# Recurrent-memory attention with a squared-ReLU feed-forward: both score masks leave TensorE

## The chip, the cores and the metric

The kernel runs on one core of a Trainium2 chip. A core has five engines with instruction queues of their own, each working in order: TensorE (PE in the profile, with its weight loads as PEld), VectorE (DVE), ScalarE (ACT), GpSimd (POOL) and SyncE (SP), which issues DMAs here. The metric is the device time of one execution in microseconds (us), lower is better; the times shown are medians of several runs.

## The reference, cut to what matters

The sequence has 2048 tokens of width 640. It is cut into 64 segments of 32 tokens, and a memory of 8 rows is carried from each segment to the next. There are 32 heads of size 128.

```python
mask = (idx[:, None] < M) | (idx[:, None] >= idx[None, :])   # idx over M + 32 = 40 rows
for s in range(n_seg):
    h = concatenate([mem, xs])                 # 8 memory rows, 32 token rows
    q, k, v = h @ Wq, h @ Wk, h @ Wv           # per head
    scores = where(mask, q @ k.T * scale, -1e9)
    o = softmax(scores) @ v @ Wo
    mem = o[:M]                                # to the next segment
    outs.append(o[M:])
h = x + concatenate(outs)                      # xs came from layernorm(x)
out = h + (relu(layernorm(h) @ w1 + b1) ** 2) @ w2 + b2
```

A memory row (the first 8 queries) sees all 40 keys; a token row sees the 8 memory keys and the tokens up to its own. Since the memory rows of a segment are the output of the one before, the 64 segments form a chain.

## The kernel before

The function `step(b, sp)` computes one segment; it is called 64 times (16 blocks of 128 tokens, 4 segments each), and then the feed-forward part follows in 4 passes of 512 tokens. All instructions are issued in the order in which the code is written, so each engine's queue is the order of the calls. Work that does not depend on the memory (projections of token rows that were known beforehand, layer norms, output projections of earlier segments) sits in lists (`fill`, `late`, `mid`, `win`) from which `run` takes pieces at fixed places of a step.

The 40 rows of a segment are handled in two parts. 32 rows, the 8 memory rows and the first 24 tokens, go through the step's own projections (`hT4`, M = 8 and HD = 24). The last 8 tokens of every segment (TL = 8, the tails) are projected elsewhere, four segments at a time, since they need not wait for the memory. `tails_in` copies their queries and keys, as columns 32 to 39, into `qT` and `kT` on POOL. In `kT` the tail's 8 keys stand four times behind one another, so that a head has 64 key columns.

The heads are worked on in four groups `g` at once: group g uses 32 partitions of the output, and four small matmuls stand side by side on TensorE. n = 0, 1 are the two halves of the heads, j = 0 to 3 the heads within group and half.

**Memory rows** (`scores`, `soft1`, `soft2`, `values`): `qz` holds, for each head, 32 query columns of which only the head's own 8 are not zero. So the 16 matmuls of `scores(n)` add up four heads' scores in one PSUM tile `sm` of 128 partitions: partition 32 g + 8 j + m is memory row m of head j in group g. The first 32 of the 64 columns are the step's own keys; the last 32 hold the tail's keys four times. Four further matmuls of an identity with `bmask` (L416) put minus 1e9 on three of the four copies, so that a row keeps copy j alone. `soft1` takes the maximum and the exponential with its sum over 64 columns (`mx`, `em`, `zm`); `soft2` takes the reciprocal `rm`, multiplies (`pm`, named pmem in the profile) and transposes 32 x 32 blocks (`pT`, named pTm). After that, copy j of the tail's probabilities lies on the partitions where the tail values of head j lie (`vt4`), and `values(n)` multiplies both parts with v and vt4 (L449, L454).

**Token rows** (`token_scores`): 32 matmuls of 40 columns write the scores of all heads into one PSUM tile `skv` of 128 x (8 x 40). Ahead of them, four matmuls of 256 columns of an identity with `mask` (L489) write the causal mask. DVE takes the maximum (L525) and subtracts it (L527), ACT takes the exponential `ek` (L542), DVE sums and takes the reciprocal (L544, L546), POOL multiplies (L548, L551), and DVE and POOL bring the result into the form (`pTk`, `pTx`) in which the next step's `token_values` uses it.

The order within a step, on TensorE: projections q0, k0, q1, k1 (L206); memory scores of half 0; 8 matmuls of the value projection's half 0; token scores of half 0; the other 12 matmuls of value half 0, which ACT then copies to `v` (L502); 8 of value half 1; memory scores and token scores of half 1; `values(0)`; the other 12 of value half 1; output projection of the memory rows and earlier tokens (`wo_rounds`, L238) with `token_values` and `values(1)` in between. On ACT stand behind each other: the copy `oT` (L215), `ek`, and `otmp` (L245); on DVE the sum `zk`, `rk` and then `o` (L246). `otmp` and `o` add up the output projection, and `mem_to_hT` (L316, L318) brings the memory rows to the next step.

PSUM tiles `sm`, `pw` and `pm` share one buffer (pool `chn`); `skv` and the projections share three (pool `mm`).

Of the kernel before, what the change touches and what calls it, by code (L numbers as in the profile page):

```python
# [8 lines left out]
ACT = mybir.ActivationFunctionType  # L9
ALU = mybir.AluOpType  # L10
AX = mybir.AxisListType
F32 = mybir.dt.float32
BF16 = mybir.dt.bfloat16
# [3 lines left out]
def kernel(  # L17
# [16 lines left out]
    nc = tc.nc  # L34
# [3 lines left out]
    SEG = 32  # L38
# [45 lines left out]
    nc.vector.memset(mhalf[:], -0.5)  # L84
    mask = const.tile([128, HG, SEG], BF16)
    nc.vector.memset(mask[:], 0.0)
    nc.gpsimd.affine_select(out=mask[0:32], in_=mask[0:32], compare_op=ALU.is_ge, fill=NEG, base=0,
                            pattern=[[0, HG], [-1, SEG]], channel_multiplier=1)
    bmask = const.tile([128, 4, TL], BF16)
    qz = const.tile([128, H, 32], BF16)  # L90
# [8 lines left out]
    nc.vector.tensor_copy(out=same[:], in_=diag[:].unsqueeze(2).to_broadcast([128, 4, TL]))  # L99
    nc.vector.tensor_scalar(out=bmask[:], in0=same[:], scalar1=-1.0, scalar2=-NEG, op0=ALU.add, op1=ALU.mult)  # L100
    qT = const.tile([128, H, NK], BF16)
    kT = const.tile([128, H, 2 * SEG], BF16)
    oT = const.tile([128, H, NK], BF16)
# [216 lines left out]
    def tails_in(b, sp, which="qk", h0=0, h1=H):  # L320
        q, k = [tails[b][w][:].rearrange("p h (k s) -> p h s k", s=4)[:, h0:h1, sp, :] if w in which else None for w in "qk"]
        if "q" in which:
            nc.gpsimd.tensor_copy(out=qT[:, h0:h1, SEG:NK], in_=q)
        if "k" in which:
            nc.gpsimd.tensor_copy(out=kT[:, h0:h1, SEG:2 * SEG].rearrange("p h (j k) -> p h j k", k=TL),  # L325
                                  in_=k.unsqueeze(2).to_broadcast([128, h1 - h0, 4, TL]))

# [52 lines left out]
    def step(b, sp, v=None):  # L380
# [32 lines left out]
        def scores(n):  # L413
            sm = chn.tile([128, 512], F32, tag="ch", name="sm")
            for g in range(G):
                nc.tensor.matmul(sm[32 * g:32 * g + 32, SEG:2 * SEG], lhsT=ident[:, 0:32],  # L416
                                 rhs=bmask[:].rearrange("p j k -> p (j k)"), start=True, stop=False, skip_group_check=True)
            for j in range(4):
                for g in range(G):
                    p = n * 16 + g * 4 + j  # L420
                    nc.tensor.matmul(sm[32 * g:32 * g + 32, 0:2 * SEG], lhsT=qz[:, p, :], rhs=kT[:, p, :],  # L421
                                     start=False, stop=(j == 3), skip_group_check=True)
            sms[n] = sm

        def soft1(n):
            mx = s2.tile([128, 1], F32, tag="mx", name="mx")
            nc.vector.tensor_reduce(out=mx[:], in_=sms[n][:, 0:2 * SEG], op=ALU.max, axis=AX.X, negate=True)
            em = s2.tile([128, 2 * SEG], BF16, tag="em", name="em")
            zm = s2.tile([128, 1], F32, tag="zm", name="zm")
            nc.scalar.activation(out=em[:], in_=sms[n][:, 0:2 * SEG], func=ACT.Exp, bias=mx[:, 0:1], scale=1.0,  # L430
                                 accum_out=zm[:])
            ems[n], zms[n] = em, zm

        def soft2(n):
            rm = s2.tile([128, 1], F32, tag="rm", name="rm")
            nc.vector.reciprocal(out=rm[:], in_=zms[n][:])
            pm = s2.tile([128, 2 * SEG], BF16, tag="pmem", name="pmem")
            nc.vector.tensor_scalar(out=pm[:], in0=ems[n][:], scalar1=rm[:, 0:1], scalar2=None, op0=ALU.mult)
            pT = s2.tile([128, 2 * SEG], BF16, tag="pTm", name="pTm")
            nc.vector.transpose(out=pT[:], in_=pm[:])  # L440
            return pT
# [44 lines left out]
        def token_scores(n):  # L486
            if n == 0:
                for g in range(G):
                    nc.tensor.matmul(skv[32 * g:32 * g + 32, :, M:NK], lhsT=ident[:, 0:32], rhs=mask[:],  # L489
                                     start=True, stop=False, skip_group_check=True)  # L490
            for j in range(4):
                for g in range(G):
                    nc.tensor.matmul(skv[32 * g:32 * g + 32, n * 4 + j, :], lhsT=qT[:, n * 16 + g * 4 + j, M:NK],  # L493
                                     rhs=kT[:, n * 16 + g * 4 + j, 0:NK], start=False, stop=(n == 1 and j == 3),
                                     skip_group_check=True)
# [26 lines left out]
        if not last:  # L522
            pT1 = soft2(1)
        mxk = s1.tile([128, HG], F32, tag="mxk", name="mxk")
        nc.vector.tensor_reduce(out=mxk[:], in_=skv, op=ALU.max, axis=AX.X)  # L525
        tk = s1.tile([128, HG, NK], F32, tag="tk", name="tk")
        nc.vector.tensor_tensor(out=tk[:], in0=skv, in1=mxk[:].unsqueeze(2).to_broadcast([128, HG, NK]), op=ALU.subtract)  # L527

# [370 lines left out]
```

## Time and profile before

| | us |
|---|---|
| median of the runs | 1021.12 |
| runs, lowest and highest | 1020.16, 1023.35 |
| the profiled execution | 1020.98 |
| its span, first to last instruction | 1018.8 |
| PE busy | 972.1 |
| DVE busy | 621.6 |
| ACT busy | 533.8 |
| POOL busy | 309.3 |

The granted clock of TensorE was 0.996 of full speed over the span. Views of the trace used here: the page; the chain of work that ended last, in order of time (each row: start, duration, engine, tile, line, how many); the timeline (start, duration, engine, line, operation, output and inputs, shapes; in brackets the engine's idle time ahead of it and what ended it); the groups by line and shape (busy us in all, mean ns of one, idle time ahead); and the waits (waiting engine, tile and line, then whom it waited for: us in all, times, longest). Matmuls overlap, and their ends are modelled, so PE's busy time includes short waits. The 64 segments take most of the span, the weights' loading some 50 us at the start, and the feed-forward part the last 140 or so.

### The profile page before, as it was taken

To read this page: it belongs to the slowest core of one execution; us is meant where nothing else is said; L and a number is where in the kernel's file an instruction comes from. 1 tells how busy PE (TensorE), PEld (TensorE's weight loads), DVE (VectorE), ACT (ScalarE), POOL (GpSimd) and SP (SyncE) were. 2 spreads that over 40 slices of the span, in tenths; PEclk is the share of its full clock that TensorE was granted. 3 is DMA by queue.
4 is the path that set the end of the run, shared out by engine and by line. 5 is a ranking of instruction groups with operands and counts; after the bars stand their busy time and mean duration, and the time that the engine had idled before them with its cause. 6 is when DMAs were issued, how large, how long until landed. Compare 5 with 4: busy or idle time off the path is not lost.

```text
span 1018.8 us, 58958 instructions
## 1 busy us (share of the span) xinstructions
PE 972.1 (95%) x26951; PEld 582.4 (57%) x26960; DVE 621.6 (61%) x1740; ACT 533.8 (52%) x1229; POOL 309.3 (30%) x803
## 2 busy tenths in 40 slices
PE   5789899999999999999999999999999998999998
PEld 2345555655655755656655666556566565555565
DVE  2256676767666667566667666666666676466432
ACT  3335555565555555555555555555555555533431
POOL 2023333333333333323333332323232343433210
PEclk9999999999999999999999999999999999999999
DMA  9960101000101010000000000000000110612200
GB/s 362 398 190 21 23 7 30 8 24 7 35 7 30 7 38 11 27 10 27 15 21 16 24 19 15 22 14 28 15 22 8 48 35 6 212 48 66 78 26 26
DMA packets 39112, 51.57 MB, mean 51 GB/s; under 512 B 5968, under 2 KB 35024, under 8 KB 36944
## 3 DMA queue, kind: packets, MB, share of 16 engines
q1 hardware_dynamic: 38080, 47.48, 14.1%
q8 instruction: 210, 3.44, 1.4%
q10 hardware_dynamic: 784, 0.34, 0.1%
q14 instruction: 38, 0.31, 0.1%
HBM read 38.37 MB, written 9.44 MB: 47 GB/s over the span
## 4 chain that ended last, share of the span: by engine, by line
PE 88%; DMA 6%; DVE 2%; issue 1%; ACT 1%; SPq 0%; DVEq 0%; POOL 0%; ACTq 0%; POOLq 0%
PE ps L206 48%; PE pw L238 15%; PE y L850 6%; PE ps L818 5%; PE ps L238 3%; DMA wk<-in_A_Wk_dram 3%; PE po L449 2%; PE po L355 2%; PE sm L421 2%; DMA wq<-in_B_w_dram 1%; DMA xt<-in_A_x_dram 1%; PE ps L493 1%; PE pm L316 1%; PE ps L489 1%; DVE o L246 1%
## 5 line engine op out<-in xcount | busy, mean ns | idle before, releaser
L206 PEld LDWEIGHTS <-hT 128*32 128x32 bf16 x7680 | 200.9, 97 | 171.6 <-issue 14.2
L238 PE MATMUL pw<-wo,oT 128*32 128x320 bf16 x4224 | 184.1, 300 | 7.1 <-issue 5.4
L206 PE MATMUL ps<-wv,hT 128*32 128x512 bf16 x2520 | 170.5, 379 | 0.9 <-ACT v L502 0.7
L206 PE MATMUL ps<-wq,hT 128*32 128x512 bf16 x2520 | 160.2, 381 | 5.3 <-DVE hT L318 5.3
L206 PE MATMUL ps<-wk,hT 128*32 128x512 bf16 x2520 | 159.5, 380 | 0.1
L238 PEld LDWEIGHTS <-oT 128*32 128x32 bf16 x4224 | 104.6, 96 | 60.5 <-ACT oT L215 13.6
L222 ACT ACTIVATE row<-ps 128x512 bf16<-128x512 f32 x156 | 93.3, 599 | 75.7 <-PE ps L206 75.1
L227 DVE STREAM_TRANSPOSE qT<-row 128x512 bf16<-128x512 bf16 x128 | 90.4, 707 | 65.8 <-ACT row L222 65.7
L548 POOL TENSOR_TENSOR pkt<-ek,rk 128x64 bf16<-128x64 bf16 x64 | 18.8, 294 | 352.5 <-DVE rk L546 352.5
L224 ACT CAST row<-ps 128x512 bf16<-128x512 f32 x115 | 68.0, 591 | 32.7 <-PE ps L206 32.5
L374 POOL COPY qz<-qT 128x96 bf16<-128x96 bf16 x126 | 33.4, 265 | 139.6 <-DVE qT L227 139.4
L325 POOL COPY kT<-kTt 128x1024 bf16<-128x1024 bf16 (+1 forms) x65 | 71.9, 1107 | 12.5 <-DVE kTt L227 12.5
L206 PEld LDWEIGHTS <-hTt 128*32 128x32 bf16 x1920 | 55.0, 97 | 32.3 <-issue 3.7
L245 ACT COPY otmp<-pw 64x320 f32<-64x320 f32 x66 | 27.9, 423 | 81.8 <-PE pw L238 81.8
L544 DVE TENSOR_REDUCE zk<-ek 128x8 f32<-128x320 bf16 x64 | 31.1, 486 | 63.5 <-ACT ek L542 63.5
L365 ACT CAST oT<-po 128x512 bf16<-128x512 f32 x128 | 68.7, 589 | 1.6
L246 DVE TENSOR_TENSOR o<-pw,otmp 64x320 bf16<-64x320 f32 x66 | 31.8, 482 | 61.6 <-ACT otmp L245 61.6
L227 DVE STREAM_TRANSPOSE kT<-row 128x512 bf16<-128x512 bf16 x65 | 46.1, 709 | 31.3 <-ACT row L224 31.3
L850 PE MATMUL y<-wq,wk 128*128 128x320 bf16 x416 | 60.9, 299 | 0.0
L405 ACT CAST row<-ps 128x256 bf16<-128x256 f32 x126 | 40.7, 375 | 31.2 <-PE ps L206 29.4
L521 ACT CAST v<-ps 128x512 bf16<-128x512 f32 x63 | 36.9, 586 | 30.7 <-PE ps L206 30.7
L502 ACT CAST v<-ps 128x512 bf16<-128x512 f32 x63 | 36.9, 586 | 30.0 <-PE ps L206 30.0
(113 smaller groups left out, 1633.6 us busy)
## 6 DMA issues: line engine op xcount, KB each, us to landing
wv<-in_A_Wv_dram SPq DMA_DIRECT2D x5, 1024.0 KB
wq<-in_A_Wq_dram SPq DMA_DIRECT2D x5, 1024.0 KB
wk<-in_A_Wk_dram SPq DMA_DIRECT2D x5, 1024.0 KB
vt<-vt_d SPq DMA_DIRECT2D x60, 64.0 KB
xt<-in_A_x_dram SPq DMA_DIRECT2D x20, 160.0 KB
vt_d<-row SPq DMA_DIRECT2D x22, 128.0 KB
wo<-in_A_Wo_dram SPq DMA_DIRECT2D x2, 1280.0 KB
wo<-in_A_Wo_dram SPq DMA_DIRECT2D x4, 640.0 KB
```

Source lines behind the costliest of these rows:

```text
L206: nc.tensor.matmul(ps[32 * k:32 * k + 32, :], lhsT=lhs(c), rhs=wr[:, c, n, k], start=(c == 0), stop=(c == DC - 1))
L222: nc.scalar.mul(out=row, in_=ps, mul=scale)
L224: nc.scalar.copy(out=row, in_=ps)
L227: nc.vector.transpose(out=dst[:, n * 16:(n + 1) * 16, 0:32], in_=row.rearrange("p (h e) -> p h e", e=32))
L238: nc.tensor.matmul(pw[32 * j:32 * j + 32, 0:DH], lhsT=lhs(p), rhs=wov2[:, head(p), ch], start=(h == 0), stop=(h == 15))
L246: nc.vector.tensor_tensor(out=o[0:64], in0=pw[0:64, 0:DH], in1=tmp[0:64], op=ALU.add)
L325: nc.gpsimd.tensor_copy(out=kT[:, h0:h1, SEG:2 * SEG].rearrange("p h (j k) -> p h j k", k=TL), in_=k.unsqueeze(2).to_broadcast([128, h1 - ...
L365: nc.scalar.copy(out=oTg[:, n, :, :, M:NK], in_=po[:, :, n * 128:(n + 1) * 128].rearrange("p g (j q) -> p g j q", q=32))
L405: nc.scalar.copy(out=row[:, u * 256:(u + 1) * 256], in_=ps[:, u * 256:(u + 1) * 256])
L502: nc.scalar.copy(out=v[:, 0:512], in_=ps0[:])
L818: nc.tensor.matmul(ps[:], lhsT=w1[:, c, fc * 128:(fc + 1) * 128], rhs=hnT[:, c, :], start=(c == 0), stop=(c == DC - 1))
L850: nc.tensor.matmul(y[:, hh, 0:DH], lhsT=f1T[:, fc, k * 128:(k + 1) * 128], rhs=w2[:, fc, cs], start=(fc == 0), stop=False, skip_group_chec ...
```

## The change

Three things are rewritten together.

1. The block mask leaves `scores`. `kT` holds the tail's keys once, so a head has 40 key columns; `scores(n)` is 16 matmuls of 40 columns, and `soft1` works on 40. The multiplication in `soft2` becomes two instructions: one over the 32 own columns, and one that repeats the tail's 8 probabilities four times and multiplies them by `rm` and by `same`, the 0/1 pattern that was there already for the token rows. The result is the `pm` of before, with zeros where the masked copies were.
2. The causal mask leaves `token_scores`. `mask` is now 128 x 40 in bf16, with zeros over the 8 memory columns. VectorE adds it, repeated over 8 heads, to the scores as it takes them out of PSUM; the maximum is then taken of the sum in SBUF.
3. The subtraction of the maximum moves from VectorE to GpSimd, in place in `tk`.

Setup changes with it: `mask` is built by a select on 32 partitions and three copies, and `bmask` is gone.

```diff
-            nc.gpsimd.tensor_copy(out=kT[:, h0:h1, SEG:2 * SEG].rearrange("p h (j k) -> p h j k", k=TL),
-                                  in_=k.unsqueeze(2).to_broadcast([128, h1 - h0, 4, TL]))
+            nc.gpsimd.tensor_copy(out=kT[:, h0:h1, SEG:NK], in_=k)
...
         def scores(n):
             sm = chn.tile([128, 512], F32, tag="ch", name="sm")
-            for g in range(G):
-                nc.tensor.matmul(sm[32 * g:32 * g + 32, SEG:2 * SEG], lhsT=ident[:, 0:32],
-                                 rhs=bmask[:].rearrange("p j k -> p (j k)"), start=True, stop=False, skip_group_check=True)
             for j in range(4):
                 for g in range(G):
                     p = n * 16 + g * 4 + j
-                    nc.tensor.matmul(sm[32 * g:32 * g + 32, 0:2 * SEG], lhsT=qz[:, p, :], rhs=kT[:, p, :],
-                                     start=False, stop=(j == 3), skip_group_check=True)
+                    nc.tensor.matmul(sm[32 * g:32 * g + 32, 0:NK], lhsT=qz[:, p, :], rhs=kT[:, p, :],
+                                     start=(j == 0), stop=(j == 3), skip_group_check=True)
...
-            nc.vector.tensor_scalar(out=pm[:], in0=ems[n][:], scalar1=rm[:, 0:1], scalar2=None, op0=ALU.mult)
+            nc.vector.tensor_scalar(out=pm[:, 0:SEG], in0=ems[n][:, 0:SEG], scalar1=rm[:, 0:1], scalar2=None, op0=ALU.mult)
+            nc.vector.scalar_tensor_tensor(out=pm[:, SEG:2 * SEG].rearrange("p (j k) -> p j k", k=TL),
+                                           in0=ems[n][:, SEG:NK].unsqueeze(1).to_broadcast([128, 4, TL]),
+                                           scalar=rm[:, 0:1], in1=same[:], op0=ALU.mult, op1=ALU.mult)
...
         def token_scores(n):
-            if n == 0:
-                for g in range(G):
-                    nc.tensor.matmul(skv[32 * g:32 * g + 32, :, M:NK], lhsT=ident[:, 0:32], rhs=mask[:],
-                                     start=True, stop=False, skip_group_check=True)
             for j in range(4):
                 for g in range(G):
                     nc.tensor.matmul(skv[32 * g:32 * g + 32, n * 4 + j, :], lhsT=qT[:, n * 16 + g * 4 + j, M:NK],
-                                     rhs=kT[:, n * 16 + g * 4 + j, 0:NK], start=False, stop=(n == 1 and j == 3),
+                                     rhs=kT[:, n * 16 + g * 4 + j, 0:NK], start=(n == 0 and j == 0), stop=(n == 1 and j == 3),
                                      skip_group_check=True)
...
+        tk = s1.tile([128, HG, NK], F32, tag="tk", name="tk")
+        nc.vector.tensor_tensor(out=tk[:], in0=skv, in1=mask[:].unsqueeze(1).to_broadcast([128, HG, NK]), op=ALU.add)
         mxk = s1.tile([128, HG], F32, tag="mxk", name="mxk")
-        nc.vector.tensor_reduce(out=mxk[:], in_=skv, op=ALU.max, axis=AX.X)
-        tk = s1.tile([128, HG, NK], F32, tag="tk", name="tk")
-        nc.vector.tensor_tensor(out=tk[:], in0=skv, in1=mxk[:].unsqueeze(2).to_broadcast([128, HG, NK]), op=ALU.subtract)
+        nc.vector.tensor_reduce(out=mxk[:], in_=tk[:], op=ALU.max, axis=AX.X)
+        nc.gpsimd.tensor_tensor(out=tk[:], in0=tk[:], in1=mxk[:].unsqueeze(2).to_broadcast([128, HG, NK]), op=ALU.subtract)
```

More of the change, by code (lines that the diff above doesn't have):

```diff
@@ L84 @@
     nc.vector.memset(mhalf[:], -0.5)
-    mask = const.tile([128, HG, SEG], BF16)
+    mask = const.tile([128, NK], BF16)
     nc.vector.memset(mask[:], 0.0)
-    nc.gpsimd.affine_select(out=mask[0:32], in_=mask[0:32], compare_op=ALU.is_ge, fill=NEG, base=0,
-                            pattern=[[0, HG], [-1, SEG]], channel_multiplier=1)
-    bmask = const.tile([128, 4, TL], BF16)
+    nc.gpsimd.affine_select(out=mask[0:32, M:NK], in_=mask[0:32, M:NK], compare_op=ALU.is_ge, fill=NEG, base=0,
+                            pattern=[[-1, SEG]], channel_multiplier=1)
+    for g in range(1, G):
+        nc.vector.tensor_copy(out=mask[32 * g:32 * g + 32], in_=mask[0:32])
     qz = const.tile([128, H, 32], BF16)
@@ L99 @@
     nc.vector.tensor_copy(out=same[:], in_=diag[:].unsqueeze(2).to_broadcast([128, 4, TL]))
-    nc.vector.tensor_scalar(out=bmask[:], in0=same[:], scalar1=-1.0, scalar2=-NEG, op0=ALU.add, op1=ALU.mult)
     qT = const.tile([128, H, NK], BF16)
-    kT = const.tile([128, H, 2 * SEG], BF16)
+    kT = const.tile([128, H, NK], BF16)
     oT = const.tile([128, H, NK], BF16)
@@ L426, in soft1 @@
             mx = s2.tile([128, 1], F32, tag="mx", name="mx")
-            nc.vector.tensor_reduce(out=mx[:], in_=sms[n][:, 0:2 * SEG], op=ALU.max, axis=AX.X, negate=True)
-            em = s2.tile([128, 2 * SEG], BF16, tag="em", name="em")
+            nc.vector.tensor_reduce(out=mx[:], in_=sms[n][:, 0:NK], op=ALU.max, axis=AX.X, negate=True)
+            em = s2.tile([128, NK], BF16, tag="em", name="em")
             zm = s2.tile([128, 1], F32, tag="zm", name="zm")
-            nc.scalar.activation(out=em[:], in_=sms[n][:, 0:2 * SEG], func=ACT.Exp, bias=mx[:, 0:1], scale=1.0,
+            nc.scalar.activation(out=em[:], in_=sms[n][:, 0:NK], func=ACT.Exp, bias=mx[:, 0:1], scale=1.0,
                                  accum_out=zm[:])
```

## The prediction

> **What bounds the kernel now.** I read the page from the top: engines, then the chain that ended last.
>
> ```profile
> span 1018.8 us, 58958 instructions
> PE 972.1 (95%) x26951; PEld 582.4 (57%) x26960; DVE 621.6 (61%) x1740; ACT 533.8 (52%) x1229; POOL 309.3 (30%) x803
> PE 88%; DMA 6%; DVE 2%; issue 1%; ACT 1%; SPq 0%; DVEq 0%; POOL 0%; ACTq 0%; POOLq 0%
> ```
>
> TensorE (PE) holds 88% of the chain, so PE time taken out of a step should shorten it, unless PE then waits for somebody else at the next meeting point. So the question is where inside a step PE meets the other engines. The chain in order of time, through the attention part of one ordinary step (columns: start, duration, what):
>
> ```profile
> 524.16 0.02 PE sm L416 x4
> 524.18 0.13 PE sm L421 x16
> 524.31 0.43 PE ps L206 x8
> 524.74 0.11 PE ps L489 x4
> 524.85 0.10 PE ps L493 x16
> 524.94 1.08 PE ps L206 x20
> 526.03 0.01 PE sm L416 x4
> 526.04 0.13 PE sm L421 x16
> 526.17 0.12 PE ps L493 x16
> 526.29 0.26 PE po L449 x16
> ```
>
> L416 and L489 are the two masks as matmuls, L421 the memory scores, L493 the token scores, L449 the first use of the memory probabilities (values of half 0). What the same stretch looks like on the other engines (timeline; the second column is the duration):
>
> ```profile
> 524.22 0.65 ACT L405 CAST row<-ps 128x256 bf16<-128x256 f32 x2 [0.48 <-PE ps L206]
> 524.62 0.77 DVE L408 STREAM_TRANSPOSE kT<-row 128x256 bf16<-128x256 bf16 x2
> 525.32 0.12 DVE L436 RECIPROCAL rm<-zm 128x1 f32<-128x1 f32 x1
> 525.47 0.24 DVE L438 TENSOR_SCALAR pmem<-em,rm 128x64 bf16<-128x64 bf16 x1
> 525.65 0.59 ACT L502 CAST v<-ps 128x512 bf16<-128x512 f32 x1 [0.47 <-PE ps L206]
> 525.75 0.24 DVE L440 STREAM_TRANSPOSE pTm<-pmem 128x64 bf16<-128x64 bf16 x1
> 526.28 0.17 PEld L449 LDWEIGHTS <-v 32*128 32x128 bf16 x16
> ```
>
> L449 needs two things: v (its weights) and pTm (its moving data). The v copy on ACT ends at 525.65 + 0.59 = 526.24 and the weight load starts 0.04 later: PE is held here by v, although the chain books the time on PE. pTm ends at 525.75 + 0.24 = 525.99; with the same 0.05 for the hand-over it has 0.25 us to spare. This is the row that decides the case.
>
> **The change, part by part.**
>
> *PE work removed.* Per step, by the chain: the block mask 0.02 + 0.01, the causal mask 0.11, and twice 16 memory scores that drop from 64 to 40 columns. The token scores have just that shape (40 columns, 16 matmuls) and take 0.10 at best against 0.13, so 2 x 0.03. Together 0.20 us a step; 63 steps make 12.6 us, if all of it arrived.
>
> The Trainium skill, page "TensorEngine Tiling (Array Packing)", section Instruction Overhead, says that each matmul has some 60 cycles of overhead, so that one column costs as much as 60. By that rule narrowing 64 columns to 40 saves only the 4 columns above 60, an estimate of 0.007 us per 16 and not the 0.03 of the rows, and the 12.6 us would be about 9.7.
>
> *How much of it reaches L449.* The v copy follows the 12th of the 20 L206 matmuls (the value projection's half 0), so only what is removed ahead of that moves v: 0.02 + 0.03 + 0.11 = 0.16 us. The 0.04 removed later, in the second memory scores, ends in the wait for v. So v allows at most 0.16 us a step: over the 61 ordinary steps 9.8 us.
>
> *The new instruction in front of pTm.* The chain to pTm does not start at anything that is removed: ACT copies the last key projection (L405), DVE transposes it (L408), then come rm, pm and pTm back to back, and the key projection stands ahead of the memory scores on PE. So pTm does not move forward when masks go; its reduction over 40 instead of 64 columns ends ahead of L408, which waits for ACT anyway, and its narrower exponential is done before DVE is free. What moves it is that pm becomes two instructions: a tensor_scalar over 32 columns and a scalar_tensor_tensor over 32 results (expand to 4 x 8, times rm, times the 0/1 pattern). Rows near them:
>
> ```profile
> L100 DVE TENSOR_SCALAR bmask<-same 128x32 bf16<-128x32 bf16 x1 | 0.2, 175 | 0.0
> L213 DVE CAST oT<-po 128x128 bf16<-128x128 f32 x63 | 18.4, 292 | 12.7 <-PE po L454 12.6
> L440 DVE STREAM_TRANSPOSE pTm<-pmem 128x64 bf16<-128x64 bf16 x126 | 30.9, 245 | 4.3
>   DVE pTm L440: 0.2, 1
> ```
>
> The last of these lines is from the view of L449's own waits: PE was held by pTm once in 62 steps. The new product has 32 results with a per-partition scalar: not under the 0.175 of a 32-column operation with constants, not over the 0.29 of a 128-column copy out of PSUM; nearest is pm itself with its scalar, 0.24, which I take for it, and 0.22 for the halved pm. The two do not depend on each other, and such neighbours overlap: the two L408 transposes take 0.77, not 2 x 0.424. So the second starts about 0.14 after the first. From pm's start to pTm's start it was 0.28; now 0.14 + 0.24 + 0.03 of hand-over = 0.41 to 0.42. pTm is 0.14 later (0.08 with 0.175, 0.19 with 0.29).
>
> *The meeting point.* pTm had 0.25 to spare and is 0.14 later: it allows L449 0.11 earlier than now, where v allows 0.16. With the hand-overs read to 0.01 I count 0.10 us a step: pTm takes v's place as what PE waits for, and half of the removed PE time is spent in that wait. If pTm could not overlap at all, the step would gain 0.03; with the shortest product it gains v's 0.16.
>
> *Behind L449* PE has fixed work, and most of its inputs have room. What is tight is the token softmax, at the end of the step.
>
> ```profile
> 526.66 0.29 DVE L213 CAST oT<-po 128x128 bf16<-128x128 f32 x1 [0.19 <-PE po L454]
> 526.94 0.16 DVE L436 RECIPROCAL rm<-zm 128x1 f32<-128x1 f32 x1
> 527.42 0.24 DVE L440 STREAM_TRANSPOSE pTm<-pmem 128x64 bf16<-128x64 bf16 x1
> 527.59 0.45 DVE L525 TENSOR_REDUCE mxk<-ps 128x8 f32<-128x320 f32 x1
> 528.07 0.49 DVE L527 TENSOR_TENSOR tk<-ps,mxk 128x320 f32<-128x320 f32 x1
> 528.37 0.29 PE L449 MATMUL po<-pTm,v 32*128 32x8 bf16 x16
> 528.99 0.47 ACT L542 ACTIVATE ek<-tk 128x320 bf16<-128x320 f32 x1
> 529.50 0.49 DVE L544 TENSOR_REDUCE zk<-ek 128x8 f32<-128x320 bf16 x1 [0.93 <-ACT ek L542]
> 530.02 0.20 DVE L546 RECIPROCAL rk<-zk 128x8 f32<-128x8 f32 x1
> 530.37 0.29 POOL L548 TENSOR_TENSOR pkt<-ek,rk 128x64 bf16<-128x64 bf16 x1 [5.34 <-DVE rk L546]
> 530.52 0.42 ACT L245 COPY otmp<-pw 64x320 f32<-64x320 f32 x1 [1.06 <-PE pw L238]
> 530.98 0.48 DVE L246 TENSOR_TENSOR o<-pw,otmp 64x320 bf16<-64x320 f32 x1 [0.76 <-ACT otmp L245]
> 531.52 0.29 PE L316 MATMUL pm<-ident,o 128*32 128x8 bf16 x20 [0.24 <-DVE o L246]
> ```
>
> Half 1's pTm ends at 527.66 and its L449 starts at 528.37: 0.7 of room, 0.6 after the change. DVE then does an add of the mask and a maximum, two operations over 320 columns as before (0.49 and 0.45 to 0.49). New is that the subtraction follows on POOL, and ACT's exponential ek, then zk and rk on DVE, wait for it. Behind ek on ACT is queued otmp, behind rk on DVE is queued o, and o feeds the next step: PE stood 0.24 us waiting for o in this very step, so a late o is paid in full. The room is 0.76, DVE's idle time ahead of o.
>
> POOL's rows of this kind:
>
> ```profile
> L548 POOL TENSOR_TENSOR pkt<-ek,rk 128x64 bf16<-128x64 bf16 x64 | 18.8, 294 | 352.5 <-DVE rk L546 352.5
> L551 POOL TENSOR_TENSOR pk<-ek,rk 128x256 bf16<-128x256 bf16 x64 | 39.4, 615 | 0.0
> L648 POOL TENSOR_TENSOR wv<-wk,wq 128x640 f32<-128x640 bf16 x12 | 18.6, 1551 | 0.0
> ```
>
> 320 elements lie between 0.615 and 1.55; on the line between those two it is 0.77, and since both operands are f32 I take 0.80, near the 256-element row. DVE to POOL takes 0.15 (rk ends 530.22, pkt starts 530.37). From half 1's pTm end to rk's end it is 2.56 now; after: -0.07 (overlap) + 0.49 + 0.03 + 0.47 + 0.15 + 0.80 + 0.05 + 0.47 + 0.03 + 0.49 + 0.03 + 0.20 = 3.14, so 0.58 more, plus 0.08 to 0.14 by which pTm itself lags PE's new schedule. rk is 0.66 to 0.72 later against a room of 0.76: just hidden. Cover gone, each 0.1 us that POOL takes over 0.85 costs up to 0.1 us in every step as tight as this one. As DVE's idle time ahead of o is 71.6 us over 78 times (0.92 in the mean), this step is on the tight side:
>
> ```profile
> DVE o L246 <- ACT otmp L245: 71.6, 78, 2.9
> ```
>
> The Trainium skill, page "GPSIMD Engine Reference", section Elementwise — side-by-side cycle accounting, gives 4497 ns for a two-input operation over 2048 fp32 elements, an estimate of 0.70 us for 320, and its section Engine selection would keep such work on VectorE; by the first figure it hides, by the second rule one would expect it to hurt, and the rows here say that it hides narrowly.
>
> *The rest.* POOL's tail copy of kT shrinks to a quarter of its elements, off the chain, and pays back there what the subtraction costs POOL. Mask building happens while the first x block and weights load. I cost these at nothing.
>
> **The sum.** 61 x 0.10 = 6.1 us. Steps 0 and 62 (no wait for v, or none for pTm) and 63 (only the causal mask) add some 0.4, and steps that have less room for pTm take as much away. The profiled execution took 1020.98 us (span 1018.8 and 2.2 around it), 0.14 under the median of the runs, 1021.12. 1020.98 - 6.1 = 1014.9, say 1015.
>
> **The rivals.**
> *v stays the bound (full gain).* The new product overlaps well or is short, and L449 moves 0.16 earlier: 61 x 0.16 + 0.5 = 10.3, so 1010.7. For it: two short DVE neighbours overlap; against it: 0.14 has to become under 0.09. 15%.
> *No change.* The product runs only after the halved pm has ended, or takes 0.3: pTm eats 0.22 to 0.25 and a step gains 0.03 or less, 1019 to 1021. For it: a new kind of instruction, none in the trace. 17%.
> *Slower: POOL ends too late.* The subtraction takes 1.1 us or more, in place with f32 on both sides. From 0.85 on o is late; the 6.1 us are used up near 1.0, and at 1.15 some 40 to 62 steps lose 0.25 to 0.3, 10 to 18 us less the 6: 1025 to 1033. For it: no row has POOL at f32 inputs, and 640 elements took 1.55. Against it: 1.1 for 320 would be half as much again per element as the 256-element row has. 14%. (It is the case that the Trainium skill's Engine selection, in "GPSIMD Engine Reference", warns of: two-input work on GpSimd at half of VectorE's speed.)
>
> **How the numbers follow.** The forecast (pTm bounds, gain of 3 to 9 us, 1012 to 1018) has 54%. About 0.3%, 3.1 us, is what a measurement of this kernel can tell from none. Faster by more: 54 + 15 less a small part, 0.66. Within: 0.19. Slower: 0.15. The range reaches from the full gain, 1010.7, into the beginning of the slow case, 1022.5.
>
> **What would show it.** In the changed kernel's trace L416 and L489 are gone, and L449's waits name pTm on DVE in most steps instead of one; pm and the product start about 0.14 apart and pTm starts 0.4 after pm; the second memory scores end earlier, but L449 only by 0.1. The subtraction on POOL lasts 0.7 to 0.9, and DVE's idle time ahead of o falls from 0.76 to about 0.1 without vanishing. I am wrong if DVE shows no idle time ahead of o (POOL came too late), if pTm is over 0.25 later, or if L449 still starts 0.04 after v.

## The result, and the profile after

| | us |
|---|---|
| before, median of 9 runs (lowest to highest) | 1020.81 (1018.40 to 1023.35) |
| after, median of 9 runs (lowest to highest) | 1016.16 (1015.05 to 1019.31) |
| after / before, 95% interval | 0.9961 (0.9945 to 0.9977) |
| the profiled execution after, its span | 1017.01, 1014.9 |

The changed kernel is 4 to 5 us faster. When it was measured again later, beside the same kernel before, the ratio was 0.9989 (0.9977 to 1.0001); that difference between two measurements of the same pair is a subject of its own below.

The page of the changed kernel: span, busy time of the engines, and the shares of the chain that ended last, by engine and by line.

```profile
span 1014.9 us, 57673 instructions
PE 957.6 (94%) x26191; PEld 564.2 (56%) x26200; DVE 629.8 (62%) x1868; ACT 536.2 (53%) x1229; POOL 311.5 (31%) x867
PE 74%; DVE 11%; DMA 7%; ACT 4%; issue 2%; SPq 1%; ACTq 0%; DVEq 0%; POOL 0%; POOLq 0%
PE ps L206 38%; PE pw L238 14%; PE y L846 5%; DVE kT L407 5%; PE ps L814 4%; PE ps L238 3%; PE po L448 2%; ACT row L404 2%; PE po L354 2%; DMA vt_d<-row 2%; DMA wq<-in_B_w_dram 2%; DVE pTm L439 2%; DVE pmem L434 1%; DMA wv<-in_A_Wv_dram 1%;
```

PE has 14.5 us less to do. More telling is the chain: PE's share fell from 88 to 74% and DVE's rose from 2 to 11%. Three DVE names are new in it, kT L407, pTm L439 and pmem L434: the way to the first values matmul now runs through half 0's probabilities. The chain in order of time shows where it leaves PE in one step:

```profile
519.76 2.19 PE ps L206 x40
521.94 0.02 issue
521.97 0.38 ACT row L404
522.35 0.02 issue
522.37 0.77 DVE kT L407 x2
523.14 0.05 DVE rm L432
523.20 0.03 issue
523.22 0.23 DVE pmem L434
523.45 0.17 DVE pmem L435
523.62 0.02 issue
523.64 0.26 DVE pTm L439
523.90 0.04 issue
523.94 0.26 PE po L448 x16
```

From the last key projection (L206) it goes to ACT's copy of the row (L404), DVE's transposition (L407), rm, the halved pm (L434), the new product (L435), the transposition pTm (L439), and back to PE at L448, the first values matmul. Before, the same stretch stood on PE from end to end. The same step on the timeline:

```profile
521.74 0.27 PE L417 MATMUL sm<-kT,qz 128*32 128x40 bf16 x16
521.84 0.60 PE L206 MATMUL ps<-wv,hT 128*32 128x512 bf16 x8
...
523.22 0.23 DVE L434 TENSOR_SCALAR pmem<-em,rm 128x32 bf16<-128x32 bf16 x1
523.25 0.58 ACT L497 CAST v<-ps 128x512 bf16<-128x512 f32 x1 [0.35 <-PE ps L206]
523.36 0.25 DVE L435 SCALAR_TENSOR_TENSOR pmem<-em,rm,same 128x32 bf16<-128x32 bf16 x1
...
523.64 0.24 DVE L439 STREAM_TRANSPOSE pTm<-pmem 128x64 bf16<-128x64 bf16 x1
523.88 0.23 PEld L448 LDWEIGHTS <-v 32*128 32x128 bf16 x16
523.94 0.26 PE L448 MATMUL po<-pTm,v 32*128 32x8 bf16 x16
...
526.44 0.72 POOL L523 TENSOR_TENSOR tk<-tk,mxk 128x320 f32<-128x320 f32 x1 [3.67 <-DVE mxk L522]
527.20 0.47 ACT L538 ACTIVATE ek<-tk 128x320 bf16<-128x320 f32 x1 [0.45 <-POOL tk L523]
```

The v copy ends at 523.25 + 0.58 = 523.83, pTm at 523.88; L448 starts 0.11 after the one and 0.06 after the other. Before, it started 0.05 after v and 0.3 after pTm. So pTm has taken v's place. Over the whole run, the groups by line and shape of what is new, and then two of the waits:

```profile
L435 DVE SCALAR_TENSOR_TENSOR pmem<-em,rm,same 128x32 bf16<-128x32 bf16 x126 | 31.0, 246 | 0.0
L434 DVE TENSOR_SCALAR pmem<-em,rm 128x32 bf16<-128x32 bf16 x126 | 29.6, 235 | 4.5
L523 POOL TENSOR_TENSOR tk<-tk,mxk 128x320 f32<-128x320 f32 x64 | 46.2, 723 | 239.9 <-DVE mxk L522 239.9
```

```profile
DVE o L246 <- ACT otmp L245: 43.2, 78, 2.6
ACT ek L538 <- POOL tk L523: 22.3, 54, 0.7
```

To compare whole runs step by step I took, for each of the 62 middle steps, the recorded starts and ends of the same instructions from the traces. V is the time from ACT's first copy of the last key row (L405 before, L404 after) to the first values matmul of half 0; "room ahead of o" is o's start less rk's end on DVE; a step's length runs from one `hT` copy (L318) to the next. Medians over the steps, in us:

```
                          before    after    difference
V                          2.072    1.977    -0.095
 values after v's end      0.055    0.111
 values after pTm's end    0.293    0.052
room ahead of o            0.759    0.298
length of a step              -        -     -0.094
```

0.094 us by 62 steps is 5.8 us.

### The profile page after: what moved, and what is told of

Read it like the earlier page. It is cut to its first block, busy times and chain, and to the rows that moved or that the text cites. A ratio compares the mean times of both kernels' runs of the same rounds, so it can differ in the third digit from the quotient of the medians.

```text
span 1014.9 us, 57673 instructions
## 1 busy us (share of the span) xinstructions
PE 957.6 (94%) x26191; PEld 564.2 (56%) x26200; DVE 629.8 (62%) x1868; ACT 536.2 (53%) x1229; POOL 311.5 (31%) x867
## 4 chain that ended last, share of the span: by engine, by line
PE 74%; DVE 11%; DMA 7%; ACT 4%; issue 2%; SPq 1%; ACTq 0%; DVEq 0%; POOL 0%; POOLq 0%
PE ps L206 38%; PE pw L238 14%; PE y L846 5%; DVE kT L407 5%; PE ps L814 4%; PE ps L238 3%; PE po L448 2%; ACT row L404 2%; PE po L354 2%; DMA vt_d<-row 2%; DMA wq<-in_B_w_dram 2%; DVE pTm L439 2%; DVE pmem L434 1%; DMA wv<-in_A_Wv_dram 1%; DMA wo<-in_A_Wo_dram 1%
## 5 line engine op out<-in xcount | busy, mean ns | idle before, releaser
L206 PEld LDWEIGHTS <-hT 128*32 128x32 bf16 x7680 | 194.9, 96 | 176.9 <-issue 14.7
L238 PE MATMUL pw<-wo,oT 128*32 128x320 bf16 x4224 | 181.9, 300 | 7.9 <-issue 3.9
L206 PE MATMUL ps<-wv,hT 128*32 128x512 bf16 x2520 | 165.2, 379 | 0.7 <-ACT v L497 0.7
L206 PE MATMUL ps<-wq,hT 128*32 128x512 bf16 x2520 | 160.0, 382 | 5.3 <-DVE hT L318 5.3
L206 PE MATMUL ps<-wk,hT 128*32 128x512 bf16 x2520 | 159.4, 381 | 0.1
L523 POOL TENSOR_TENSOR tk<-tk,mxk 128x320 f32<-128x320 f32 x64 | 46.2, 723 | 239.9 <-DVE mxk L522 239.9
L206 PEld LDWEIGHTS <-hTt 128*32 128x32 bf16 x1920 | 53.3, 96 | 31.5 <-issue 0.8
L516 ACT CAST v<-ps 128x512 bf16<-128x512 f32 x63 | 36.9, 585 | 39.2 <-PE ps L206 39.2
L404 ACT CAST row<-ps 128x256 bf16<-128x256 f32 x126 | 40.8, 375 | 30.0 <-PE ps L206 30.0
L822 ACT ACTIVATE wv<-ps,b1f 128x512 bf16<-128x512 f32 (+1 forms) x56 | 37.6, 672 | 27.3 <-PE ps L814 26.9
L417 PEld LDWEIGHTS <-qz 128*32 128x32 bf16 x2016 | 34.3, 95 | 31.2 <-POOL qz L373 2.0
```

The lines of the kernel that those rows point to most:

```text
L206: nc.tensor.matmul(ps[32 * k:32 * k + 32, :], lhsT=lhs(c), rhs=wr[:, c, n, k], start=(c == 0), stop=(c == DC - 1))
L238: nc.tensor.matmul(pw[32 * j:32 * j + 32, 0:DH], lhsT=lhs(p), rhs=wov2[:, head(p), ch], start=(h == 0), stop=(h == 15))
L404: nc.scalar.copy(out=row[:, u * 256:(u + 1) * 256], in_=ps[:, u * 256:(u + 1) * 256])
L523: nc.gpsimd.tensor_tensor(out=tk[:], in0=tk[:], in1=mxk[:].unsqueeze(2).to_broadcast([128, HG, NK]), op=ALU.subtract)
L822: nc.scalar.activation(out=r[:, 0:w], in_=ps[:, 0:w], func=ACT.Relu, bias=b1f[:, fc:fc + 1], scale=1.0)
```

## The experiments

The question was whether the step works as I said (half 0's probabilities against the v copy, with the subtraction on POOL just hidden), and whether the time follows the step. The rivals were that the narrower work on PE was what counted wherever it stood, that POOL's subtraction held something back, and that the measured difference had little to do with the step. All ratios are to the kernel before, measured in the same job. Some kernels here have other line numbers, as lines were added; the names stay. The table has V, its change against before, the change of a step's length times 62, and what was measured; the runs are told of below it.

| run | V | change of V | step x 62 | ratio to before (95%) | measured |
|---|---|---|---|---|---|
| after, first result | 1.977 | -0.095 | -5.8 | 0.9961 (0.9945 to 0.9977) | -4.0 |
| e1_block_back | 1.961 | -0.111 | -6.9 | 0.9953 (0.9937 to 0.9969) | -4.8 |
| e2_block_only | 2.029 | -0.043 | -3.0 | 1.0015 (1.0001 to 1.0029) | +1.5 |
| e3_half0 | 1.978 | -0.094 | -6.8 | 0.9947 (0.9929 to 0.9964) | -5.4 |
| e4_half1 | 1.961 | -0.111 | -7.0 | 0.9964 (0.9950 to 0.9978) | -3.7 |
| e5_sub_dve | 1.977 | -0.095 | -6.6 | 0.9989 (0.9979 to 1.0000) | -1.1 |
| e6_sub_twice | 1.977 | -0.095 | +13.0 | 1.0164 (1.0148 to 1.0180) | +16.7 |
| e7_before_v_first | 2.009 | -0.063 | -3.9 | 0.9977 (0.9967 to 0.9987) | -2.3 |
| e8_half1_v_first | 1.867 | -0.205 | -13.0 | 0.9909 (0.9895 to 0.9923) | -9.2 |
| f1_after | 1.978 | -0.094 | -5.8 | 0.9989 (0.9977 to 1.0001) | -1.1 |
| f2_before_pad | 2.072 | 0.000 | -0.1 | 1.0026 (1.0015 to 1.0036) | +2.6 |
| f3_after_pad | 1.978 | -0.094 | -5.9 | 0.9967 (0.9954 to 0.9979) | -3.4 |
| f4_e8_pad | 1.867 | -0.205 | -12.7 | 0.9911 (0.9897 to 0.9926) | -9.1 |

"Measured" is (ratio - 1) times the median of the kernel before in that job (1020.81, 1014.56, 1015.52 and 1017.46 us; the e and f runs fall into three jobs, e1 to e4, e5 to e8 and f1 to f4, each on another chip). The same kernel before differs by 0.6% between the jobs, so that only ratios can be compared.

### One mask at a time

e1_block_back is the changed kernel with the block mask back on PE in both halves; only the causal mask has left. (WIDE holds the halves that keep 64 columns and the mask matmuls.)

```diff
+    WIDE = (0, 1)
...
+            wide = n in WIDE
+            nk = 2 * SEG if wide else NK
+            for g in range(G if wide else 0):
+                nc.tensor.matmul(sm[32 * g:32 * g + 32, SEG:2 * SEG], lhsT=ident[:, 0:32],
+                                 rhs=bmask[:].rearrange("p j k -> p (j k)"), start=True, stop=False, skip_group_check=True)
...
+            if n in WIDE:
+                nc.vector.tensor_scalar(out=pm[:], in0=ems[n][:], scalar1=rm[:, 0:1], scalar2=None, op0=ALU.mult)
+            else:
```

> The block mask goes back to TensorE for both halves (64 key columns, pm in one instruction again); only the causal mask stays on VectorE and GpSimd. Theory (in the changed kernel half 0's pTm sets the first values matmul; with the old pm it has its 0.25 us of room back, and the v copy sets it, 0.11 us earlier than in the kernel before): first values matmul 0.11 us earlier per step than before, against 0.094 in the changed kernel; 61 x 0.11 = 6.7 us under the kernel before, so as fast as the changed kernel or up to 1 us faster, though 0.09 us of TensorE work per step is back. Rival (what counts is TensorE work removed): 0.11 of the 0.20 us, so 4.65 x 0.55 = 2.6 us under the kernel before, 2 us slower than the changed kernel.

Its timeline, in a step:

```profile
519.57 0.59 ACT L510 CAST v<-ps 128x512 bf16<-128x512 f32 x1 [0.37 <-PE ps L209]
519.78 0.24 DVE L452 STREAM_TRANSPOSE pTm<-pmem 128x64 bf16<-128x64 bf16 x1
520.21 0.17 PEld L461 LDWEIGHTS <-v 32*128 32x128 bf16 x16
```

v ends at 520.16 and the weight load of the values follows 0.05 later, while pTm has been there since 520.02: with the single pm in half 0, v binds as before, and the whole 0.11 us of the causal mask arrives. So the causal mask alone gives the step more (0.111) than both masks together (0.095).

e2_block_only is the opposite: only the block mask leaves PE, and the causal mask's matmuls and VectorE's subtraction are as before.

```diff
+            if n == 0:
+                for g in range(G):
+                    nc.tensor.matmul(skv[32 * g:32 * g + 32, :, M:NK], lhsT=ident[:, 0:32], rhs=mask[:],
+                                     start=True, stop=False, skip_group_check=True)
...
-        nc.vector.tensor_reduce(out=mxk[:], in_=tk[:], op=ALU.max, axis=AX.X)
-        nc.gpsimd.tensor_tensor(out=tk[:], in0=tk[:], in1=mxk[:].unsqueeze(2).to_broadcast([128, HG, NK]), op=ALU.subtract)
+        nc.vector.tensor_reduce(out=mxk[:], in_=skv, op=ALU.max, axis=AX.X)
+        tk = s1.tile([128, HG, NK], F32, tag="tk", name="tk")
+        nc.vector.tensor_tensor(out=tk[:], in0=skv, in1=mxk[:].unsqueeze(2).to_broadcast([128, HG, NK]), op=ALU.subtract)
```

> Only the block mask leaves TensorE (40 columns, the 0/1 pattern in pm); the causal mask stays as matmuls and the subtraction on VectorE. Theory: the v copy allows 0.04 to 0.05 us per step (only what is removed ahead of it counts, the first memory scores), pTm allows 0.09, so v still sets the first values matmul, 0.04 earlier: 2.5 us under the kernel before. Rival (removed TensorE work counts): 0.09 of 0.20, 2.1 us by the changed kernel's rate and 5.5 in full. Rival (the longer pm alone costs): no gain or slower.

V fell by 0.043, as expected, with v still binding (values 0.055 after v's end, 0.104 after pTm's). The two parts alone make 0.111 + 0.043 = 0.154, against 0.095 for both together: 0.06 us of each step is lost where they meet, in half 0's probabilities. But e2's time is 1.5 us longer where its steps are shorter. The step's theory missed that time, which is what the second rival had (the longer pm alone costs); the steps speak against that rival's cause, as pTm is there 0.104 before the values and V is shorter.

### Which half

The block mask can be replaced by the pattern in one half only. e3_half0 does it in half 0, e4_half1 in half 1; the causal mask is on VectorE in both.

```diff
+    WIDE = (1,)      # e3_half0
+    WIDE = (0,)      # e4_half1
```

> As the changed kernel, but the 0/1 pattern in half 0 alone; half 1 has its block mask matmuls and 64 columns back. Theory: half 0's pTm sets the first values matmul as in the changed kernel (0.094 us earlier than before), and half 1's TensorE work was hidden in that wait: within 1 us of the changed kernel. Rival (removed work counts): 0.045 us per step back, 1 to 2.8 us slower than the changed kernel.

> As the changed kernel, but the 0/1 pattern in half 1 alone; half 0 has its block mask matmuls and 64 columns back. Theory: the v copy sets the first values matmul, 0.11 us earlier than before (half 0's pm is short again, half 1's has 0.6 us of room): 6.7 us under the kernel before, so up to 1 us faster than the changed kernel. Rival (the pattern's product costs in either half): as the 0/1 pattern in half 0 alone.

By V they come out apart as the theory has it: with the pattern in half 0 V is what it is in the changed kernel (values 0.052 after pTm), and with the pattern in half 1 alone it is e1's (0.055 after v). The page says it at a glance. These are the engines' shares of the chain of e1, e3 and e4:

```profile
PE 89%; DMA 5%; DVE 2%; ACT 2%; issue 1%; SPq 1%; ACTq 0%; DVEq 0%; POOL 0%; POOLq 0%
```

```profile
PE 77%; DVE 11%; DMA 5%; ACT 4%; issue 2%; SPq 1%; ACTq 0%; DVEq 0%; POOL 0%; POOLq 0%
```

```profile
PE 86%; DMA 7%; DVE 3%; ACT 2%; SPq 1%; issue 1%; ACTq 0%; DVEq 0%; POOL 0%; POOLq 0%
```

DVE has 11% of the chain in the two kernels that have the product in half 0 (e3 and the changed one) and 2 to 3% in those that don't. In half 1 the product costs nothing that shows, as pTm has time there: e4's steps are as short as e1's. (e3's steps are 0.016 shorter than the changed kernel's at the same V. By the medians o starts at the same time in both, 6.67 after ACT's copy of the row, so the difference arises behind o; its cause is open.) The ratios (0.9953, 0.9947 and 0.9964) don't separate the three: what differs between them by the step is 0.2 us a run, under the measurement. That half 0's product is what costs is shown by V and by the chain, not by the time.

### Where the subtraction runs

e5_sub_dve is the changed kernel with the subtraction on VectorE again.

```diff
-        nc.gpsimd.tensor_tensor(out=tk[:], in0=tk[:], in1=mxk[:].unsqueeze(2).to_broadcast([128, HG, NK]), op=ALU.subtract)
+        nc.vector.tensor_tensor(out=tk[:], in0=tk[:], in1=mxk[:].unsqueeze(2).to_broadcast([128, HG, NK]), op=ALU.subtract)
```

> As the changed kernel, but the maximum is subtracted on VectorE. Theory (GpSimd's 0.72 us are covered: VectorE still idles 0.3 us ahead of o in the median step): the same time within 1 us, while the idle time ahead of o goes back up by about 0.35. Rival (the late exponential costs somewhere): 1 to 3 us faster than the changed kernel.

The room ahead of o goes back up from 0.298 to 0.520, and V stays. So rk ends 0.22 later with POOL's subtraction than with VectorE's, and V doesn't feel it; the steps are 0.012 us shorter with VectorE's, 0.8 us in all, which the time doesn't show. Its ratio, 0.9989, is that of the second measurement of the changed kernel.

e6_sub_twice lets POOL subtract a second time, zeros, which changes no value.

```diff
+        nc.gpsimd.tensor_tensor(out=tk[:], in0=tk[:], in1=none8[:].unsqueeze(2).to_broadcast([128, HG, NK]), op=ALU.subtract)
```

> As the changed kernel, with a second subtraction (of zeros) on GpSimd behind the first, which changes no value: the exponential comes 0.65 to 0.72 us later. Theory (0.19 to 0.3 us of room in most steps, and a late o is paid): o comes 0.3 to 0.5 us late in some 40 steps, 10 to 19 us slower than the changed kernel. Rival (o has cover of its own in the lists of side work): under 3 us slower.

The timeline of a step, and then its waits over the run:

```profile
523.47 0.72 POOL L525 TENSOR_TENSOR tk<-tk,mxk 128x320 f32<-128x320 f32 x1 [3.71 <-DVE mxk L524]
524.28 0.72 POOL L526 TENSOR_TENSOR tk<-tk,none 128x320 f32<-128x320 f32 x1
525.03 0.47 ACT L541 ACTIVATE ek<-tk 128x320 bf16<-128x320 f32 x1 [1.22 <-POOL tk L526]
526.05 0.20 DVE L545 RECIPROCAL rk<-zk 128x8 f32<-128x8 f32 x1
526.17 0.47 DVE L248 TENSOR_TENSOR o<-pw,otmp 64x320 bf16<-64x320 f32 x1
```

```profile
ACT ek L541 <- POOL tk L526: 70.3, 63, 1.5
DVE o L248 <- ACT otmp L247: 17.1, 19, 2.5
```

The second one starts 0.81 after the first. rk and o now stand back to back (526.05 and 526.17), in 55 of 62 steps; DVE's idle time ahead of o is down from 43.2 us over 78 times to 17.1 over 19, and ACT's wait for POOL up from 22.3 to 70.3. A step became 0.30 us longer than in the changed kernel, 19 us in all, and the time 18 to 21 us (1.0164 against 0.9989 and 0.9961). So the threshold is there. By the medians ek came 0.80 later, o 0.48 later, and the step became 0.30 longer: 0.5 us of the delay was absorbed, 0.3 ahead of o and the rest behind it. The changed kernel lies under the threshold by 0.3 to 0.5 us.

### What v cost

e7_before_v_first is the kernel before with nothing but an order changed: the token scores of half 0, with their mask, stand behind the 12 matmuls of the value projection and the v copy, no longer ahead of them.

```diff
-        token_scores(0)
-        if ready:
-            run(fill, DC)
         if not ready:
             proj(wv, "half", lhs, 0, ps0, 2, DC)
             nc.scalar.copy(out=v[:, 0:512], in_=ps0[:])
+        token_scores(0)
+        if ready:
+            run(fill, DC)
```

> The kernel before, with one move: the first token scores, their mask with them, come behind the 12 matmuls of the value projection's half 0 and its v copy, so that v is ready 0.21 us earlier. No work is added or removed. Theory (in the kernel before the first values matmul waits for v, some 0.06 us beyond what TensorE itself needs): 0.06 us per step, 3.5 us under the kernel before. Rival (the constant distance to the v copy is chance, and TensorE's own work sets it): no change.

In a step of its timeline:

```profile
523.79 0.58 ACT L499 CAST v<-ps 128x512 bf16<-128x512 f32 x1 [0.27 <-PE ps L206]
524.10 0.24 DVE L440 STREAM_TRANSPOSE pTm<-pmem 128x64 bf16<-128x64 bf16 x1
524.57 0.17 PEld L449 LDWEIGHTS <-v 32*128 32x128 bf16 x16
```

v is there at 524.37 and pTm at 524.34, both 0.2 before the weight load: PE now arrives last. The 0.063 us by which V fell is what the wait for v cost in the kernel before, though the page of before counts it as busy PE.

e8_half1_v_first puts together what these runs point to: the causal mask on VectorE, the pattern in half 1 only, and the v copy ahead of the token scores.

```diff
+    WIDE = (0,)
...
-        token_scores(0)
-        if ready:
-            run(fill, DC)
         if not ready:
             proj(wv, "half", lhs, 0, ps0, 2, DC)
             nc.scalar.copy(out=v[:, 0:512], in_=ps0[:])
+        token_scores(0)
+        if ready:
+            run(fill, DC)
```

> The causal mask on VectorE and GpSimd, the 0/1 pattern in half 1 alone, and the v copy moved ahead as in the run before. Theory: v allows 0.21 us per step against the kernel before, TensorE's own work 0.06 + 0.11 + 0.04 = 0.21, half 0's pTm 0.24: 0.21 x 61 = 12.8 us under the kernel before, 8 us under the changed kernel. Rival (another wait stands close behind): between 6.7 and 10 us under the kernel before.

The same three rows of its timeline:

```profile
515.18 0.58 ACT L507 CAST v<-ps 128x512 bf16<-128x512 f32 x1 [0.27 <-PE ps L209]
515.49 0.24 DVE L452 STREAM_TRANSPOSE pTm<-pmem 128x64 bf16<-128x64 bf16 x1
515.82 0.17 PEld L461 LDWEIGHTS <-v 32*128 32x128 bf16 x16
```

v ends at 515.76, pTm at 515.73 and the values start 0.06 and 0.09 later: PE, v and pTm meet within 0.1 us. V is 0.205 shorter than before. This kernel is faster than both: 1006.96 us against 1015.52 for the kernel before in its job.

### Time that is in no step

Two measurements stood against the step: e2 (+1.5 where -3.0 was due) and e5 (-1.1 where -6.6 was due). Others gained less than was expected of them, though their steps came out as expected: e1 4.8 us in place of 6.7, e4 3.7 in place of 6.7, e7 2.3 in place of 3.5, and e8 9.2 in place of 12.8, which is in the range of its rival. Four runs followed. f1_after is the changed kernel once more, with no edit. The other three are the kernel before, the changed one and e8, each with 66 pairs of a weight load and a small matmul ahead of the first projection, whose result nobody uses:

```diff
+    for _ in range(3):
+        pz = mmtile()
+        for i in range(22):
+            nc.tensor.matmul(pz[0:32, 0:8], lhsT=ident[:, 0:32], rhs=ident[:, 0:8], start=True, stop=True)
```

> The changed kernel once more, unchanged, beside the three others on one chip. Per step it should repeat 0.094 us less up to the first values matmul. In time 4 to 6 us under the kernel before.

> The kernel before with 66 extra pairs of weight load and matmul (8 columns, result unused) ahead of the first projection, where TensorE waits for weights anyway: 132 instructions more, so that all later TensorE code stands at another place of the instruction stream. Nothing in a step changes. Theory (the runs so far gained 1 to 4 us less than their medians per step say, because stalls marked 'issue', in which an engine waits for nothing that the profile shows, fall differently in each program): 1 to 4 us slower than the kernel before, or at least different by over 1 us, with the same median step. Rival (the place of the code does not matter): within 0.5 us, and the shortfall has another cause.

> The changed kernel with the same 66 pairs ahead. Theory of the place of the code: differs from the changed kernel without them by over 1 us in either direction, with the same median step. Rival: within 0.5 us.

> The fastest version so far (causal mask on VectorE and GpSimd, 0/1 pattern in half 1 alone, v copy first) with the same 66 pairs ahead. Per step 0.205 us less than the kernel before up to the first values matmul, as without the pairs; 7 to 13 us under the kernel before, and by the theory of the place of the code over 1 us away from the 9.2 it had.

The groups of the padded kernel before show what the pairs take; by the view of their line they run from 11.4 to 13.2 us.

```profile
L735 PE MATMUL ps<-ident 128*32 128x8 bf16 x66 | 1.9, 168 | 0.0
```

They lie where PE waits for the first weights: the first `hT` copy of the loop is at 61.7 us with them and at 62.0 without. V is 2.072 to the last digit. Yet the kernel before got slower by 2.6 us and the changed one faster by 2.2 (0.9967 against 0.9989 in the same job), while e8 stayed where it was (0.9911 against 0.9909 in the earlier job), where more than 1 us had been expected: a miss for the idea that any shift of the code moves the time. f1, where 4 to 6 us less had been expected, gained 1.1: another miss.

Setting all thirteen ratios against the steps gives a plainer picture. Measured less step x 62 is, from the table's top: +1.8, +2.1, +4.5, +1.4, +3.3, +5.5, +3.7, +1.6, +3.8, +4.7, +2.7, +2.5, +3.6. All are positive, their mean is 3.2 and their standard deviation 1.3; they rest on four measurements of the kernel before. The same offset, 2.7, stands at the kernel before once it has the pairs and no other change. So it need not be a cost of the change. The reading that fits is that the kernel before, as it stands, is some 3 us faster than its steps let expect, and that each of the other kernels here lost that; with one padded copy of the kernel before it is argued and not shown. Against the padded kernel before, the padded changed one is 0.9967 / 1.0026 = 0.9941, 6.0 us less, and the changed one without pairs 0.9989 / 1.0026 = 0.9963, 3.8 us less; the steps say 5.8.

What this offset consists of is not settled. Part of it may lie in V. In every profile V is 0.2 to 2.0 us above its median in a few steps, the fourth and the last of the 62 among them; the sum of V exceeds 62 medians by 1.5 us in the kernel before, by 2.9 in the padded one, by 3.2 and 2.8 in the two profiles of the changed kernel, and by 1.7 to 3.5 in the others. The profiles also have idle time marked "issue" on PE, for which the trace shows no cause. A single step differs by -1.3 to +0.9 us between the kernel before and the changed one, but by -0.6 to +0.5 between the two profiles of the changed kernel too (the 62 steps together 802.5 and 799.3 us), so that one profile of each can't say where 3 us went. Nor did I test another size of padding.

## Why the prediction was right or wrong

**The meeting point, right.** v was the bound before (e7: 0.063 us a step), pTm is the bound after (0.052 behind it in place of 0.293), and L449, now L448, comes 0.095 us earlier, where I had counted 0.10. e1 and e4 show the 0.11 of the case in which v stays the bound with half 0 untouched, and e3 that it is half 0's product that takes the rest.

**The DVE terms, right.** The product takes 246 ns (I took 0.24), the halved pm 235 (0.22); they start 0.14 apart, pTm starts 0.42 after pm (0.41 to 0.42), and it comes 0.147 later than before (0.14).

**The PE work removed, partly wrong.** "Take 0.10 at best against 0.13, so 2 x 0.03" failed. I read 0.13 from a row of the chain, whose ends are modelled. By starts, the 16 scores of 64 columns are followed 0.11 later by the next matmul, those of 40 columns 0.10 later (in the timeline of after above, 521.74 to 521.84). The timeline of the kernel before:

```profile
524.02 0.29 PE L421 MATMUL sm<-kT,qz 128*32 128x64 bf16 x16
524.13 0.60 PE L206 MATMUL ps<-wv,hT 128*32 128x512 bf16 x8
```

Over the steps that have all 16 recorded the medians are 0.113 and 0.104: narrowing saves 0.009. The Trainium skill, page "TensorEngine Tiling (Array Packing)", section Instruction Overhead, has about 60 cycles as the least that a matmul costs, from which I had worked out 0.007; the starts agree with it and not with my 0.03. The block mask itself was larger than its row, 0.028 and not 0.02 or 0.01. Together 2 x 0.009 + 2 x 0.028 + 0.109 = 0.183 us a step in place of 0.20, and what lies ahead of v is 0.146 by starts (e1 and e2 together: 0.154) in place of 0.16. As pTm binds, the forecast didn't depend on it: that this term was three times too large did no harm, and that was luck.

**POOL, right in kind, too high in size.** 0.80 was forecast and 0.722 measured. (The Trainium skill, page "GPSIMD Engine Reference", section Elementwise — side-by-side cycle accounting, led to an estimate of 0.70, which the row is nearer to.) DVE idles 0.30 ahead of o in the median step, 0.19 at least in the first profile (0.15 in f1's), where I had said "about 0.1". The subtraction is hidden, as e5 shows, and a subtraction that is too slow does cost, as e6 shows, but the edge lies 0.3 to 0.5 us away and not 0.05 to 0.1.

**What would show it, wrong as to the view.** "L449's waits name pTm on DVE in most steps" did not come true: the view of waits names pTm once in the changed kernel too. The wait is there. From the last matmul ahead of the values to the values it takes 0.120 us in e7, where PE arrives last, 0.183 in the kernel before and 0.275 in the changed one: waits of 0.06 and 0.155. Part of them lies under the modelled end of that last matmul, after which only 0.085 of idle time is left in the changed kernel. It was the chain that showed pTm.

**The sum, right for the steps, with a term missing for the time.** 61 x 0.10 = 6.1 became 5.8. The measured gain is 4.0 by the ratio (4.65 by the medians) in the first result and 1.1 when measured again. What lacks in the sum is an offset, 1.8 us in the first result and about 3 in the mean of all runs, which, if the padded control is taken at its word, belongs to the kernel before and not to the change. It is about as large as the 0.3% that I had taken for the measurement's limit, so whether the change clears 0.3% is not certain: one measurement of the pair says yes, the other no. The mechanism and its 0.10 us a step were right; that the first measured time came so near to the forecast is in part luck.

## What to carry to other kernels

Work taken from the busiest engine is worth only what the next meeting point lets through; write down for each input of that point how long it waits, and charge an inserted instruction to the input whose chain it lengthens. Here the same rewrite is free in half 1, where the chain has room, and costs 0.06 of 0.15 us in half 0; leaving half 0 alone and bringing the v copy forward (e8) doubled what the step gained. Where a change is worth less than half a per cent, compare distances between the same instructions, step by step, and measure a version of the old kernel with idle padding as a second base (one size of padding was tried here).

## What was not expected of the hardware

- 66 pairs of a weight load and a matmul in idle time at the start, 1.9 us in all, moved the kernel before by +0.26% (0.15 to 0.36) without a change in the median step, the changed kernel by -0.22% and e8, whose two measurements are from different jobs, by nothing.
- A column-tiled matmul of 64 columns costs hardly more than one of 40: 16 of them 0.113 us against 0.104.
- A wait of PE of 0.06 us a step, in the kernel before, stays invisible as a wait and is counted as busy; e7 made it visible by removing it.
- Two short DVE instructions that don't depend on each other start 0.14 us apart, though each takes 0.235 to 0.246. (This one was in the forecast, from the L408 rows.)
